# Six more stretches of zero-matmuls in chunks 0 and 1 of a fused attention and SoLU kernel, and five wide ones in place of eighteen narrow ones

## The chip, the cores and the metric

The kernel runs on one core of a Trainium2 chip. A core has five engines that run side by side and wait for each other through semaphores: TensorE (PE in the profile; its weight loads are shown apart as PEld), VectorE (DVE), ScalarE (ACT), GpSimd (POOL) and SyncE (SP). The last two also issue most of the DMA transfers. The metric is the device time of one execution in microseconds; lower is better.

## What is computed

The reference is linear attention with a norm per head, followed by a two-layer network with a SoLU and a layer norm. Batch 8, 8 heads, 576 positions, head width 64, so 4608 tokens of width 512, and 1024 hidden columns:

```python
kv  = einsum('bhsd,bhse->bhde', k, v)
o   = einsum('bhsd,bhde->bhse', q, kv)
x   = o / sqrt(mean(o*o, -1) + 1e-6) * g_norm          # then laid out as (4608, 512)
h   = x @ w_in                                         # (4608, 1024)
u   = h * softmax(h)
ln  = (u - mean(u)) / sqrt(var(u) + 1e-6) * g_ln
out = ln @ w_out                                       # (4608, 512)
```

## The kernel before, in words

The work is cut into nine chunks. Chunks 0 to 7 are 512 positions of one batch each, chunk 8 gathers the last 64 positions of all batches. A chunk goes through these pieces, named in the kernel as `name.chunk.part`:

- `q`, `k`, `v`: loads, issued by POOL (L317). Chunks 0 and 1 come in two halves. The first half of chunk 0 is loaded by SP (L327) and cast by DVE and ACT (L231).
- `qT_mm` (L415): PE turns q; `qT` (L231): a copy of it out of PSUM.
- `kv_mm` (L377): 72 small products of k and v per half; `kv` (L231): copies of the result.
- `o_mm` (L443): 8 products of q and kv; `sq` (L235): ACT squares the result; `s_mm` (L507): one product with `head_mean`, the mean over a head; `ex` (L521 in chunk 0; `ln`, `ex` at L511 and L515 from chunk 1): the reciprocal root on ACT; `x` (L527): DVE multiplies. Each is done for two halves `hf` and two parts `z`, as `s_mm.0.1.0`.
- `h` (L582 in chunks 0 to 3, L611 later): products with `w_in`. Then `exp` on ACT (L589, L619), `u` on DVE (L593, L625), squares and sums on POOL, and `out` (L759): the products with `w_out`, scaled and stored.
- Once per run, `w_mean` (L740) and `w_center` (L745) fold the layer norm into `w_out`, whose two halves POOL loads (L346). `w_in` is loaded at L341.

The order in which every piece is issued is written out by hand, in one list, `ORDER`. The framework adds the waits. Each engine works through its own pieces in this order, so a piece that waits holds up everything behind it on the same engine. PSUM has eight banks; `HOME` gives each PSUM tile (`s.0.0.1`, `h.0.7` and so on) its bank. A tile may be written when every reader of the bank's previous tile is done.

`warm.N` pieces are zero-matmuls: TensorE multiplies a tile of zeros into a PSUM tile that the piece behind it will overwrite. `FILL` lists them as (tile, how many, columns). Those with 512 columns run at L822. `warm.1`, on the tile of q's first turn by PE after the first products of k and v, is 18 transposes of 128 columns (L817). Before the change there are seven such pieces: 19 and 8 wide matmuls ahead of the first data (`warm.6`, `warm.3`, `warm.2`, `warm.0`), `warm.1`, one wide matmul at `warm.4` and one at `warm.5`.

Of the kernel before, what the change touches and what calls it, by code (L numbers as in the profile page):

```python
# [22 lines left out]
o_mm.0.0 q_last.0:act sq.0.0.1 kv.0.1.1 kv.0.1.0 s_mm.0.0.1 sq.0.0.0 ex.0.0.1 o_mm.0.1 sq.0.1.1 sq.0.1.0 g_ln  # L23
s_mm.0.0.0 x.0.0.1 v.1.1 ex.0.0.0 s_mm.0.1.1 ex.0.1.1 x.0.0.0 x.0.1.1 w_out.0 s_mm.0.1.0 qT_mm.1.0 qT.1.0 w_out.1
q.2.0 k.2.0 ex.0.1.0 x.0.1.0 v.2.0 kv_mm.1.0 kv.1.0.1:act kv.1.0.0:act h.0.7.0 table h.0.1.0 warm.5 h.0.4.0 o_mm.1.0
sq.1.0.0 sq.1.0.1 k.3.0 h.0.5.0 g_mean h.0.6.0 h.0.4.1 exp.0.4 u.0.4 usq.0.4 h.0.1.1 exp.0.1 h.0.6.1 u.0.1 usq.0.1
h.0.5.1 exp.0.5 es.0.2 u.0.5 usq.0.5 exp.0.6 u.0.6 h.0.0.0 h.0.0.1 exp.0.0 u.0.0 q.3.0 usq.0.0 s_mm.1.0.1 ln.1.0.1
ex.1.0.1 qT_mm.1.1 qT.1.1 usq.0.6 x.1.0.1 h.0.2.0 h.0.2.1 exp.0.2 u.0.2 s_mm.1.0.0 ln.1.0.0 ex.1.0.0 h.0.7.1 exp.0.7
es.0.3 kv_mm.1.1 kv.1.1.1 kv.1.1.0 x.1.0.0 h.0.3.0 h.0.3.1 exp.0.3 u.0.3 es.0.0 es.0.1 usq.0.3 o_mm.1.1 sq.1.1.1
usq.0.2 u.0.7 usq.0.7 sq.1.1.0 w_mean.0 s_mm.1.1.1 ln.1.1.1 ex.1.1.1 s_mm.1.1.0 ln.1.1.0 v.3.0 w_mean.1 x.1.1.1  # L30
w_center.0 h.1.0.0 h.1.7.0 h.1.3.0 v.5.0 ex.1.1.0 x.1.1.0 w_center.4 h.1.1.0 h.1.2.0 h.1.2.1 exp.1.2 w_center.2
qT_mm.2.1 qT_mm.2.0 h.1.3.1 k.5.0 u.1.2 usq.1.2 w_center.3 qT.2.1:act v.4.0 qT.2.0:act h.1.7.1 exp.1.7 w_center.1
w_center.5 h.1.1.1 exp.1.1 u.1.1 h.1.5.0 h.1.5.1 h.1.4.0 exp.1.5 exp.1.3 h.1.6.0 h.1.6.1 h.1.0.1 exp.1.0 u.1.5 k.4.0
es.1.1 usq.1.5 es.1.0 q.4.0 u.1.7 usq.1.7 h.1.4.1 u.1.0 kv_mm.2.0 kv.2.1.1 exp.1.6 es.1.3 exp.1.4 kv.2.0.0
kv.2.1.0:act u.1.4 k.6.0 w_center.6 u.1.6 kv.2.0.1:act w_center.7 kv.2.1.2:act out.0.2.0 kv.2.0.2:act out.0.3.0
out.0.3.1 out.0.3.2 usq.1.4:act u.1.3 usq.1.3 o_mm.2.0 sums.0 sq.2.0.1 s_mm.2.0.1 es.1.2 sq.2.0.0 v.6.0 s_mm.2.0.0
usq.1.6 ln.2.0.0 ln.2.0.1 ex.2.0.0 turn.0 stats.0 rstd.0 out.0.2.1 out.0.2.2 out.0.2.3 ob.0.2 store.0.2 o_mm.2.1
sq.2.1.0 sq.2.1.1 x.2.0.0 out.0.0.0 out.0.0.1 out.0.0.2 out.0.3.3 ob.0.3:act usq.1.0 store.0.3 out.0.0.3 ob.0.0
store.0.0 ex.2.0.1 s_mm.2.1.0 qT_mm.3.1 kv_mm.3.0 kv.3.0.1 k.7.0 x.2.0.1 ln.2.1.0 v.7.0 kv.3.1.1:act kv.3.1.0
kv.3.0.2:act kv.3.1.2 ex.2.1.0 x.2.1.0 out.0.1.0 out.0.1.1 kv.3.0.0:act s_mm.2.1.1 ln.2.1.1 out.0.1.2 out.0.1.3 ob.0.1  # L40
usq.1.1 ex.2.1.1 h.2.7.0 x.2.1.1 qT_mm.3.0 qT.3.0:act h.2.5.0 q_last.3:act h.2.4.0 h.2.0.0 h.2.0.1 exp.2.0 q_last.1
h.2.3.0 h.2.6.0 h.2.3.1 exp.2.3 h.2.7.1 qT.3.1 u.2.0 kv_mm.5.0 kv.5.1.0 kv.5.0.1:act q.5.0 exp.2.7 kv.5.0.2:act
kv.5.0.0:act h.2.4.1 exp.2.4 store.0.1 kv.5.1.1:act q.6.0 qT.5 u.2.3 u.2.7 kv.5.1.2 h.2.2.0 h.2.2.1 exp.2.2 usq.2.7
h.2.1.0 h.2.1.1 u.2.2 usq.2.0 h.2.6.1 u.2.4 o_mm.3.1 out.1.2.0 usq.2.2 out.1.2.1 exp.2.1 es.2.0 u.2.1 sq.3.1.0 exp.2.6
u.2.6 s_mm.3.1.0 ln.3.1.0 ex.3.1.0 sums.1 turn.1 stats.1 q_last.4 h.2.5.1 sq.3.1.1 out.1.3.0 q_last.2 g_all s_mm.3.1.1
kv_mm.4.0 exp.2.5 x.3.1.0 u.2.5 ln.3.1.1 es.2.1 usq.2.6 kv.4.0.0:act kv.4.0.2 kv.4.1.1 rstd.1 usq.2.5 ob.1.2 kv.4.0.1
ex.3.1.1 x.3.1.1 o_mm.3.0 sq.3.0.0 usq.2.4:act es.2.2 out.1.1.0 usq.2.1 kv.4.1.2:act out.1.3.1 ob.1.3 store.1.3 es.2.3
qT_mm.4.1 qT.4.1 sq.3.0.1 kv.4.1.0:act out.1.0.0 s_mm.3.0.0 ln.3.0.0 ex.3.0.0 out.1.1.1 ob.1.1 s_mm.3.0.1 o_mm.4.1
qT_mm.4.0 ln.3.0.1 ex.3.0.1 x.3.0.0 store.1.2 x.3.0.1 out.1.0.1 qT.4.0 kv_mm.6.0 kv.6.1.1 kv.6.1.0 ob.1.0 sq.4.1.1
store.1.0 kv.6.1.2 kv.6.0.2 s_mm.4.1.1 ln.4.1.1 h.3.5.1 exp.3.5 u.3.5 sq.4.1.0 h.3.2.1 exp.3.2 u.3.2 usq.3.2 h.3.4.1  # L50
exp.3.4 u.3.4 h.3.0.1 kv.6.0.1:act ex.4.1.1 x.4.1.1 exp.3.0 u.3.0 kv.6.0.0 s_mm.4.1.0 ln.4.1.0 h.3.1.1 exp.3.1 usq.3.5
h.3.6.1 kv_mm.7.0 kv.7.1.0 kv.7.0.1:act kv.7.1.2:act usq.2.3 kv.7.0.0:act u.3.1 store.1.1 o_mm.4.0 sq.4.0.0 kv.7.0.2
exp.3.6 kv.7.1.1 h.3.3.1 h.3.7.1 exp.3.3 u.3.3 out.2.2.0 out.2.2.1 es.3.1 sq.4.0.1 s_mm.4.0.1 exp.3.7 es.3.3 u.3.6
ex.4.1.0 x.4.1.0 ln.4.0.1 ex.4.0.1 u.3.7 usq.3.7:act s_mm.4.0.0 ln.4.0.0 ex.4.0.0 x.4.0.1 qT.6 out.2.0.0 sums.2
out.2.3.0 o_mm.5.0 es.3.2 turn.2 stats.2 rstd.2 x.4.0.0 o_mm.5.1 sq.5.1.0 sq.5.0.1 out.2.0.1 usq.3.4 ob.2.0 sq.5.0.0
out.2.3.1 ob.2.2 store.2.2 ob.2.3 s_mm.5.1.0 ln.5.1.0 ex.5.1.0 x.5.1.0 h.4.1.0 expt.4.1.0 s_mm.5.0.0 ln.5.0.0 sq.5.1.1
out.2.1.0 out.2.1.1 ob.2.1 ex.5.0.0 usq.3.0 es.3.0 x.5.0.0 h.4.3.0 expt.4.3.0 usq.3.3 s_mm.5.0.1 ln.5.0.1 ex.5.0.1
usq.3.6 usq.3.1 sums.3 ut.4.3.0 ut.4.1.0 turn.3 store.2.1 s_mm.5.1.1 h.4.2.0 bn.4.3.0 stats.3 q.7.0 qT.7 x.5.0.1
ln.5.1.1 ex.5.1.1 x.5.1.1 expt.4.2.0 out.3.3.0 ut.4.2.0 bn.4.2.0 rstd.3 out.3.3.1 o_mm.6.0 sq.6.2 sq.6.0 ob.3.3:act
ssum.6.0 o_mm.6.1 bn.4.1.0 h.4.2.1 q_last.7 sq.6.3 expt.4.2.1 ut.4.2.1 sq.6.1 out.3.2.0 out.3.2.1 ob.3.2 h.4.3.1  # L60
sred.6.0 expt.4.3.1 h.4.1.1 expt.4.1.1 ssum.6.1 ut.4.3.1 ut.4.1.1 rh.6.0 turnu.4.1 rg.6.0 out.3.0.0 out.3.0.1
ob.3.0:act h.4.0.1 sred.6.1 rg.6.2 o_mm.7.1 rh.6.1 sq.7.1 bn.4.2.1 xt.6.0 xt.6.2 h.4.0.0 expt.4.0.1 expt.4.0.0 rg.6.3
out.3.1.0 sq.7.3 ut.4.0.1 out.3.1.1 ut.4.0.0 ob.3.1:act bn.4.0.0 rg.6.1 xt.6.1 store.3.2 xt.6.3 x.6 turnu.4.0 h.5.2.1
h.5.0.0 ssum.7.1 sred.7.1 expt.5.2.1 ut.5.2.1 expt.5.0.0 ut.5.0.0 h.5.0.1 store.2.0 expt.5.0.1 h.5.1.1 expt.5.1.1
out.4.3.0 h.5.1.0 ut.5.0.1 bn.4.1.1 out.4.3.1 bn.4.3.1 rh.7.1 q_last.6:act expt.5.1.0 rg.7.3 ut.5.1.1 rg.7.1
q_last.5:act qT.8 xt.7.3 xt.7.1 h.5.3.1 expt.5.3.1 bn.4.0.1 o_mm.7.0 ut.5.1.0 ut.5.3.1 out.4.2.0 sq.7.0 sq.7.2 h.5.2.0
# [798 lines left out]
```

## Time and profile before

| | us |
|---|---|
| three runs | 184.80, 184.79, 186.75; median 184.80 |
| the profiled execution, its own time | 186.39 |
| its span in the trace | 184.3 |
| PE busy | 172.2 |
| ACT busy | 135.6 |
| DVE busy | 133.4 |
| POOL busy | 98.1 |
| mean granted TensorE clock | 0.978 |

The profile is of one execution, and its times are counted from the start of the span; 186.39 - 184.3 = 2.1 us lie around the span. In a line of the timeline stand the start, the duration, the engine, the line of the kernel, the operation with its output and inputs, how many instructions were merged, and in brackets the idle time before with what ended it. "issue" there means that the profile shows nothing that the engine waited for. The granted clock is the share of its full speed at which TensorE ran. A matmul's duration includes its way through the array, so that of several in a row the distance between two starts is the price, and not the duration of one.

### The profile page before, as it was taken

What the parts mean: (1) busy time and instruction counts of PE and PEld (TensorE: products, weight loads), DVE (VectorE), ACT (ScalarE), POOL (GpSimd) and SP (SyncE); (2) the same over time, 40 slices, a digit from 0 to 9 for tenths busy, and PEclk for the clock granted to TensorE, in tenths of its full rate; (3) what the DMA queues carried; (4) which work ended last, traced back from release to release, by engine and by line L of the source; (5) the groups of instructions that cost most, each with busy time, mean ns of one, the idle gap of its engine ahead of it and who ended that gap; (6) DMA issues with size and microseconds to landing.
All of it is one profiled execution on the core that took longest, in us unless ns stands there. A gap on an engine that the chain in (4) does not pass through costs nothing.

```text
span 184.3 us, 5088 instructions
## 1 busy us (share of the span) xinstructions
PE 172.2 (93%) x2072; PEld 83.9 (46%) x2072; DVE 133.4 (72%) x277; ACT 135.6 (74%) x279; POOL 98.1 (53%) x112
## 2 busy tenths in 40 slices
...
PEclk9999569999999999999999999999999999999998
...
GB/s 182 292 217 207 207 322 312 208 207 201 208 210 229 270 213 208 208 199 166 215 103 66 177 136 173 55 227 179 219 247 77 252 261 171 230 144 206 215 233 201
DMA packets 56140, 37.10 MB, mean 201 GB/s; under 512 B 37549, under 2 KB 49333, under 8 KB 56117
## 3 DMA queue, kind: packets, MB, share of 16 engines
...
q8 instruction: 16, 0.26, 0.5%
...
## 4 chain that ended last, share of the span: by engine, by line
PE 57%; DVE 9%; DMA 3%; ACT 2%; POOL 1%; issue 1%; POOLq 0%; ACTq 0%
PE out_ps L759 22%; PE h_ps L611 17%; PE h_ps L582 8%; DMA w_sb<-u_sb 3%; DVE bn_sb L631 3%; DVE u_sb L625 2%; PE misc_ps L377 2%; PE misc_ps L693 2%; PE s_ps L507 2%; PE o_ps L443 1%; PE o_ps L457 1%; PE misc_ps L415 1%; POOL es_sb L472 1%; DVE x_sb L527 1%; DVE w_out_sb L745 1%; ACT rst_sb L235 1%
## 5 line engine op out<-in xcount | busy, mean ns | idle before, releaser
L611 PE MATMUL h_ps<-w_in_sb,x_sb 128*128 128x512 bf16 x160 | 38.0, 379 | 0.4 <-DVE usq_sb L495 0.4
L759 PE MATMUL out_ps<-w_out_sb,w_sb 128*128 128x512 bf16 (+1 forms) x168 | 36.9, 369 | 0.3 <-DMA w_sb<-u_sb 0.3
L237 POOL TENSOR_TENSOR usq_sb<-u_sb 128x512 bf16<-128x512 bf16 x29 | 29.7, 1041 | 12.2 <-PE s_ps L507 6.5
L582 PE MATMUL h_ps<-x_sb,w_in_sb 128*128 128x512 bf16 x128 | 32.3, 396 | 2.6 <-DVE x_sb L527 2.6
L619 ACT ACTIVATE e_sb<-h_ps,zero_t 128x512 f32<-128x512 f32 x40 | 27.2, 686 | 8.6 <-PE h_ps L611 7.9
L759 PE MATMUL out_ps<-w_out_sb,u_sb 128*128 128x512 bf16 x128 | 31.0, 379 | 0.0
L593 DVE TENSOR_TENSOR u_sb<-h_ps,e_sb 128x512 bf16<-128x512 f32 x32 | 20.8, 684 | 11.0 <-ACT e_sb L589 10.9
L625 DVE TENSOR_TENSOR u_sb<-h_ps,e_sb 128x512 bf16<-128x512 f32 x40 | 26.0, 679 | 1.6 <-ACT e_sb L619 1.6
L631 DVE BATCH_NORM_STATS2 bn_sb<-u_sb 128x6 f32<-128x512 bf16 x40 | 25.8, 680 | 0.2
L759 PEld LDWEIGHTS <-w_sb 128*128 128x128 bf16 x168 | 16.3, 98 | 18.7 <-DMA w_sb<-u_sb 0.8
L527 DVE SCALAR_TENSOR_TENSOR x_sb<-o_ps,g_cols,rst_sb 128x512 bf16<-128x512 f32 x24 | 18.8, 795 | 7.9 <-ACT rst_sb L515 3.8
L589 ACT ACTIVATE e_sb<-h_ps,zero_t 128x512 f32<-128x512 f32 x32 | 20.6, 690 | 4.7 <-PE h_ps L582 4.6
L611 PEld LDWEIGHTS <-x_sb 128*128 128x128 bf16 x160 | 15.4, 97 | 19.0 <-issue 1.2
L606 POOL TENSOR_TENSOR es_sb<-e_sb 128x512 bf16<-128x512 f32 x16 | 20.3, 1275 | 2.2 <-ACT e_sb L589 2.2
L582 PEld LDWEIGHTS <-w_in_sb 128*128 128x128 bf16 x128 | 12.3, 100 | 17.9 <-issue 6.1
L235 ACT ACTIVATE osq_sb<-o_ps,zero_t 128x512 bf16<-128x512 f32 x24 | 15.5, 681 | 5.5 <-PE o_ps L443 5.4
L759 PEld LDWEIGHTS <-u_sb 128*128 128x128 bf16 x128 | 11.8, 98 | 14.1 <-issue 0.8
L488 POOL TENSOR_TENSOR lss_sb<-rh_sb,g_all 128x512 f32<-128x512 f32 x12 | 12.2, 1041 | 7.9 <-ACT rh_sb L484 7.9
L472 POOL TENSOR_TENSOR es_sb<-rst_sb 128x512 f32<-128x512 bf16 x6 | 6.9, 1155 | 15.4 <-ACT rst_sb L235 9.0
L511 ACT ACTIVATE lss_sb<-s_ps,eps_t 128x512 f32<-128x512 f32 x20 | 13.6, 684 | 1.7 <-PE s_ps L507 1.6
L515 ACT ACTIVATE rst_sb<-lss_sb,zero_t 128x512 f32<-128x512 f32 x20 | 14.5, 723 | 0.5
L231 DVE CAST kvd<-misc_ps 64x128 bf16<-64x128 f32 (+1 forms) x23 | 6.3, 286 | 8.7 <-PE misc_ps L377 7.4
...
## 6 DMA issues: line engine op xcount, KB each, us to landing
...
w_sb<-in_moe_w_out_dram POOLq DMA_DIRECT2D x2, 1024.0 KB, 15.4
...
```

What stands on the lines that cost most here:

```text
L235: nc.scalar.activation(out=dst, in_=src, func=AF.Square, bias=zero_t[:, :])
L237: on[engine].tensor_tensor(out=dst, in0=src, in1=src, op=MUL)
L527: nc.vector.scalar_tensor_tensor(out=t[:, z, 2 * hf:2 * hf + 2].rearrange("p a (vt w) -> p w (a vt)", w=2), in0=T["o", c, hf, z].rearrange ...
L582: nc.tensor.matmul(bank(("h", c, f), [128, 512])[:, :], w_in_sb[:, dt, f * 128:(f + 1) * 128], T["x", c][:, :, dt, :], start=(dt == 0), st ...
L589: nc.scalar.activation(out=t[:, f % 2, :], in_=T["h", c, f][:, :], func=AF.Exp, bias=zero_t[:, :])
L593: nc.vector.tensor_tensor(out=t[:, f, :], in0=T["h", c, f][:, :], in1=T["e", c, f // 2][:, f % 2, :], op=MUL)
L606: on[engine].tensor_tensor(out=t[:, n, :], in0=e[:, 0, :], in1=e[:, 1, :], op=ADD)
L611: nc.tensor.matmul(bank(("h", c, m, g), [128, 512])[:, :], x[:, NP * (m ^ 2 * odd(c, dt)) + dt, :] if c in TOKA else x[:, m // 2 ^ odd(c, ...
L619: nc.scalar.activation(out=t[:, g, :], in_=T["h", c, m, g][:, :], func=AF.Exp, bias=zero_t[:, :], accum_out=se[:, m, g:g + 1])
L625: nc.vector.tensor_tensor(out=t[:, m, g * 512:(g + 1) * 512], in0=T["h", c, m, g][:, :], in1=T["e", c, m][:, g, :], op=MUL)
L631: nc.vector.bn_stats(out=t[:, m, g, :], in_=T["u", c][:, m, g * 512:(g + 1) * 512])
L759: nc.tensor.matmul(bank(key, [128, d_model])[:, cols], T["w", c][:, m, f, :] if c in TOKS else T["u", c][:, f, m * 128:(m + 1) * 128], w_o ...
```

## The change

Six pieces `warm.7` to `warm.12` are added, each ahead of a piece that waits: 4 wide matmuls ahead of `s_mm.0.0.1`, 2 ahead of `s_mm.0.1.1`, 1 ahead of `s_mm.0.1.0`, 4 ahead of `h.0.7.0`, 1 ahead of `s_mm.1.1.1` and 3 ahead of `h.1.1.0`. `warm.1` becomes 5 wide matmuls and no longer needs the identity. The order of all other pieces stays word for word. The homes of many PSUM tiles are renumbered. The tiles of the k and v products are declared as whole banks, and the copies read the same part of them as before.

```diff
 ORDER (only the places with a new word; the rest is the same sequence)
-... kv.0.1.1 kv.0.1.0 s_mm.0.0.1 sq.0.0.0 ex.0.0.1 o_mm.0.1 ...
+... kv.0.1.1 kv.0.1.0 warm.7 s_mm.0.0.1 sq.0.0.0 ex.0.0.1 o_mm.0.1 ...
-... ex.0.0.0 s_mm.0.1.1 ex.0.1.1 x.0.0.0 x.0.1.1 w_out.0 s_mm.0.1.0 qT_mm.1.0 ...
+... ex.0.0.0 warm.8 s_mm.0.1.1 ex.0.1.1 x.0.0.0 x.0.1.1 w_out.0 warm.12 s_mm.0.1.0 qT_mm.1.0 ...
-... kv.1.0.1:act kv.1.0.0:act h.0.7.0 table h.0.1.0 warm.5 h.0.4.0 o_mm.1.0 ...
+... kv.1.0.1:act kv.1.0.0:act warm.9 h.0.7.0 table h.0.1.0 warm.5 h.0.4.0 o_mm.1.0 ...
-... w_mean.0 s_mm.1.1.1 ... w_center.4 h.1.1.0 ...
+... w_mean.0 warm.10 s_mm.1.1.1 ... w_center.4 warm.11 h.1.1.0 ...

-FILL = {0: ("s.warm", 19, 512), 1: ("misc.qT.0.0", 18, 128), 2: ("o.0.0.1", 5, 512), ...}
+FILL = {0: ("s.warm", 19, 512), 1: ("misc.qT.0.0", 5, 512), 2: ("o.0.0.1", 5, 512), ...
+        7: ("s.0.0.1", 4, 512), 8: ("s.0.1.1", 2, 512), 9: ("h.0.7", 4, 512), 10: ("s.1.1.1", 1, 512),
+        11: ("h.1.1", 3, 512), 12: ("s.0.1.0", 1, 512)}

 def kv_mm, kv_copy:
-    bank(kv_key(b, x, w), [128, 2, D])          ... T[kv_key(b, x, part)][:, :, :]
+    bank(kv_key(b, x, w), [128, 8, D])          ... T[kv_key(b, x, part)][:, 0:2, :]

 def warm(key, n, cols):
     if kind == "qT":
-        t = bank(key, [128, 2, 4, 128], BF16)
-        for i in range(n):
-            nc.tensor.transpose(t[:, 0, i % 4, :], zeros[:, 0:128], ident[:, :])
-        return
+        flat = bank(key, [128, 2, 4, 128], BF16).rearrange("p n y t -> p (n y t)").bitcast(FP32)
...
     for _ in range(n):
         nc.tensor.matmul(flat[:, 0:cols], zeros[:, :], zeros[:, None, :].to_broadcast([128, cols // 128, 128]), start=True, stop=True)
```

Followed through the list, the renumbering gives eight tiles another predecessor in their bank: `s.0.0.1` now follows `kv.0.1.1` in place of `kv.0.1.0`, `o.0.1.0` the other way round, `h.0.1` follows `o.0.1.0`, `o.1.0.0` follows `qT.1.0`, `o.1.0.1` follows `kv.1.0.1`, `h.0.5` follows `s.0.1.0`, `h.1.2` follows `o.1.1.0` and `qT.2.1` follows `s.1.0.0`.

More of the change, by code (lines that the diff above doesn't have):

```diff
@@ L22 @@
 kv.0.0.1:act warm.1 k.1.0 qT.0.1:act gs w_in.0 w_in.1 k.1.1 ld.q q.0.0 qT_mm.0.0 warm.4 q.1.1 qT.0.0 kv_mm.0.1 turn_g
[L23 to L66, printed above, removed]
@@ new lines @@
+s_mm.0.0.0 x.0.0.1 v.1.1 ex.0.0.0 warm.8 s_mm.0.1.1 ex.0.1.1 x.0.0.0 x.0.1.1 w_out.0 warm.12 s_mm.0.1.0 qT_mm.1.0
+qT.1.0 w_out.1 q.2.0 k.2.0 ex.0.1.0 x.0.1.0 v.2.0 kv_mm.1.0 kv.1.0.1:act kv.1.0.0:act warm.9 h.0.7.0 table h.0.1.0
+warm.5 h.0.4.0 o_mm.1.0 sq.1.0.0 sq.1.0.1 k.3.0 h.0.5.0 g_mean h.0.6.0 h.0.4.1 exp.0.4 u.0.4 usq.0.4 h.0.1.1 exp.0.1
+h.0.6.1 u.0.1 usq.0.1 h.0.5.1 exp.0.5 es.0.2 u.0.5 usq.0.5 exp.0.6 u.0.6 h.0.0.0 h.0.0.1 exp.0.0 u.0.0 q.3.0 usq.0.0
+s_mm.1.0.1 ln.1.0.1 ex.1.0.1 qT_mm.1.1 qT.1.1 usq.0.6 x.1.0.1 h.0.2.0 h.0.2.1 exp.0.2 u.0.2 s_mm.1.0.0 ln.1.0.0
@@ new lines @@
+h.1.6.1 h.1.0.1 exp.1.0 u.1.5 k.4.0 es.1.1 usq.1.5 es.1.0 q.4.0 u.1.7 usq.1.7 h.1.4.1 u.1.0 kv_mm.2.0 kv.2.1.1 exp.1.6
+es.1.3 exp.1.4 kv.2.0.0 kv.2.1.0:act u.1.4 k.6.0 w_center.6 u.1.6 kv.2.0.1:act w_center.7 kv.2.1.2:act out.0.2.0
+kv.2.0.2:act out.0.3.0 out.0.3.1 out.0.3.2 usq.1.4:act u.1.3 usq.1.3 o_mm.2.0 sums.0 sq.2.0.1 s_mm.2.0.1 es.1.2
+sq.2.0.0 v.6.0 s_mm.2.0.0 usq.1.6 ln.2.0.0 ln.2.0.1 ex.2.0.0 turn.0 stats.0 rstd.0 out.0.2.1 out.0.2.2 out.0.2.3
+ob.0.2 store.0.2 o_mm.2.1 sq.2.1.0 sq.2.1.1 x.2.0.0 out.0.0.0 out.0.0.1 out.0.0.2 out.0.3.3 ob.0.3:act usq.1.0
@@ new lines @@
+h.2.2.1 exp.2.2 usq.2.7 h.2.1.0 h.2.1.1 u.2.2 usq.2.0 h.2.6.1 u.2.4 o_mm.3.1 out.1.2.0 usq.2.2 out.1.2.1 exp.2.1
+es.2.0 u.2.1 sq.3.1.0 exp.2.6 u.2.6 s_mm.3.1.0 ln.3.1.0 ex.3.1.0 sums.1 turn.1 stats.1 q_last.4 h.2.5.1 sq.3.1.1
+out.1.3.0 q_last.2 g_all s_mm.3.1.1 kv_mm.4.0 exp.2.5 x.3.1.0 u.2.5 ln.3.1.1 es.2.1 usq.2.6 kv.4.0.0:act kv.4.0.2
+kv.4.1.1 rstd.1 usq.2.5 ob.1.2 kv.4.0.1 ex.3.1.1 x.3.1.1 o_mm.3.0 sq.3.0.0 usq.2.4:act es.2.2 out.1.1.0 usq.2.1
+kv.4.1.2:act out.1.3.1 ob.1.3 store.1.3 es.2.3 qT_mm.4.1 qT.4.1 sq.3.0.1 kv.4.1.0:act out.1.0.0 s_mm.3.0.0 ln.3.0.0
@@ new lines @@
+ex.3.0.0 out.1.1.1 ob.1.1 s_mm.3.0.1 o_mm.4.1 qT_mm.4.0 ln.3.0.1 ex.3.0.1 x.3.0.0 store.1.2 x.3.0.1 out.1.0.1 qT.4.0
+kv_mm.6.0 kv.6.1.1 kv.6.1.0 ob.1.0 sq.4.1.1 store.1.0 kv.6.1.2 kv.6.0.2 s_mm.4.1.1 ln.4.1.1 h.3.5.1 exp.3.5 u.3.5
+sq.4.1.0 h.3.2.1 exp.3.2 u.3.2 usq.3.2 h.3.4.1 exp.3.4 u.3.4 h.3.0.1 kv.6.0.1:act ex.4.1.1 x.4.1.1 exp.3.0 u.3.0
+kv.6.0.0 s_mm.4.1.0 ln.4.1.0 h.3.1.1 exp.3.1 usq.3.5 h.3.6.1 kv_mm.7.0 kv.7.1.0 kv.7.0.1:act kv.7.1.2:act usq.2.3
+kv.7.0.0:act u.3.1 store.1.1 o_mm.4.0 sq.4.0.0 kv.7.0.2 exp.3.6 kv.7.1.1 h.3.3.1 h.3.7.1 exp.3.3 u.3.3 out.2.2.0
```

121 lines of the change are left out of this document (75 added, 46 removed).

## The prediction, made before the result was known

> **What bounds the kernel now.** I read the page first (busy shares, then the granted clock in 40 slices of 4.6 us), then busy time by window, then the timeline of the early part.
>
> ```profile
> span 184.3 us, 5088 instructions
> PE 172.2 (93%) x2072; PEld 83.9 (46%) x2072; DVE 133.4 (72%) x277; ACT 135.6 (74%) x279; POOL 98.1 (53%) x112
> PEclk9999569999999999999999999999999999999998
> ```
>
> TensorE is busy for 172 of 184 us. Its clock is whole but for the fifth and sixth slice. The windows carry start and end, length, then busy us of PE, PEld, DVE, ACT, POOL, then the clock:
>
> ```profile
> 12.17:15.58 3.41, 2.27 (x91) 1.18 (x88) 1.25 (x4) 1.79 (x3) 1.47 (x2) 1.00 1.21 207
> 15.58:19.00 3.42, 2.09 (x29) 1.07 (x31) 1.50 (x3) 2.47 (x5) 1.48 (x2) 1.00 1.14 212
> 19.00:22.41 3.41, 2.33 (x75) 1.46 (x71) 2.59 (x5) 2.40 (x4) 0.74 (x1) 0.50 1.15 206
> 22.41:25.82 3.41, 3.41 (x16) 0.96 (x15) 0.00 (x0) 0.99 (x2) 1.48 (x2) 0.50 1.22 255
> 80.00:110.00 30.00, 30.00 (x435) 14.82 (x434) 24.31 (x51) 28.68 (x56) 17.24 (x18) 1.00 0.80 151
> ```
>
> The clock is at half from 19.00 to 25.82 us. It fell behind a stretch in which TensorE was busy for 2.09 of 3.42 us, held behind one with 2.27 of 3.41, and came back behind one that was full. From 80 to 110 us TensorE has no gap, so what it does earlier in the first 60 us is still earlier there. What matters lies between 10 and 40 us:
>
> ```profile
> 10.53 1.18 PE L817 MATMUL misc_ps<-ident,zeros 128*128 128x128 bf16 x18
> 11.66 0.62 PE L415 MATMUL misc_ps<-ident,q_sb 128*128 128x128 bf16 x8
> 13.32 0.41 PE L443 MATMUL o_ps<-qT_sb,kvd 64*64 64x256 bf16 x8
> 14.52 0.38 PE L507 MATMUL s_ps<-osq_sb,head_mean 128*128 128x512 bf16 x1 [0.79 <-ACT osq_sb L235]
> 14.83 0.40 PE L443 MATMUL o_ps<-qT_sb,kvd 64*64 64x256 bf16 x5
> 16.07 0.30 PE L443 MATMUL o_ps<-qT_sb,kvd 64*64 64x256 bf16 x3 [0.83 <-issue]
> 16.30 0.39 PE L507 MATMUL s_ps<-osq_sb,head_mean 128*128 128x512 bf16 x1
> 17.15 0.38 PE L507 MATMUL s_ps<-osq_sb,head_mean 128*128 128x512 bf16 x1 [0.46 <-ACT osq_sb L235]
> 17.72 0.38 PE L507 MATMUL s_ps<-osq_sb,head_mean 128*128 128x512 bf16 x1 [0.20 <-ACT osq_sb L235]
> 18.88 1.11 PE L377 MATMUL misc_ps<-v_sb,k_sb 64*64 64x64 bf16 x71 [0.19 <-ACT rst_sb L521]
> 21.07 1.86 PE L582 MATMUL h_ps<-x_sb,w_in_sb 128*128 128x512 bf16 x4 [1.08 <-DVE x_sb L527]
> 22.73 0.63 PE L822 MATMUL h_ps<-zeros 128*128 128x512 bf16 x1
> 23.16 1.06 PE L582 MATMUL h_ps<-x_sb,w_in_sb 128*128 128x512 bf16 x2
> 24.14 0.64 PE L443 MATMUL o_ps<-qT_sb,kvd 64*64 64x256 bf16 x8
> 24.71 4.16 PE L582 MATMUL h_ps<-x_sb,w_in_sb 128*128 128x512 bf16 x16
> 33.41 1.19 PE L740 MATMUL out_ps<-w_sb,g_mean 128*128 128x512 f32 x4
> 34.91 0.38 PE L507 MATMUL s_ps<-osq_sb,head_mean 128*128 128x512 bf16 x1 [0.31 <-ACT osq_sb L235]
> 39.20 1.46 PE L582 MATMUL h_ps<-x_sb,w_in_sb 128*128 128x512 bf16 x6 [0.95 <-DVE x_sb L527]
> ```
>
> The six new pieces stand in the bracketed waits of 0.79, 0.46, 0.20, 1.08, 0.31 and 0.95 us. The seventh gap, 0.83 us inside `o_mm.0.1`, has no releaser: five of eight products ran, and the sixth came 1.1 us later.
>
> **The change, part by part.** The price of one wide matmul at full clock, and of `o_mm`, from the chain of what ended last:
>
> ```profile
> 59.72 3.45 PE h_ps L582 x16
> 66.57 0.34 PE o_ps L443 x8
> ```
>
> A wide one is 3.45 / 16 = 0.216 us. Zero-matmuls have the same shape.
>
> *warm.1.* Eighteen transposes fill 10.53 to 11.66, 1.13 us; five wide ones take 1.08. The next piece waits for its q behind them either way. Zero.
>
> *The renumbered banks.* Of the eight tiles with another predecessor, `s.0.0.1` and `o.0.1.0` swap two copies that both end by 13.76 (first row below), `h.0.1` and `h.1.2` now need an x that the product of h just ahead of them on PE awaits already, and the others need an earlier reader. Zero. The whole-bank tiles read and write what they did. Zero.
>
> ```profile
> 13.27 0.49 DVE L231 CAST kvd<-misc_ps 128x128 bf16<-128x128 f32 x2 [0.26 <-PE misc_ps L377]
> 18.28 1.47 DVE L527 SCALAR_TENSOR_TENSOR x_sb<-o_ps,g_cols,rst_sb 128x512 bf16<-128x512 f32 x2 [1.84 <-ACT rst_sb L521]
> 19.64 0.69 DVE L231 COPY qT_sb<-misc_ps 128x1024 bf16<-128x1024 bf16 x1
> 20.23 0.79 DVE L527 SCALAR_TENSOR_TENSOR x_sb<-o_ps,g_cols,rst_sb 128x512 bf16<-128x512 f32 x1
> 16.41 1.26 ACT L235 ACTIVATE osq_sb<-o_ps,zero_t 128x512 bf16<-128x512 f32 x2 [0.78 <-PE o_ps L443]
> 19.17 0.69 ACT L521 ACTIVATE rst_sb<-s_ps,eps_t 128x512 f32<-128x512 f32 x1 [0.34 <-DVE x_sb L527]
> ```
>
> *The fills themselves*, at full clock. `warm.7`: 4 x 0.216 = 0.86 from 13.73 (end of `o_mm.0.0`) is 14.59, against a start of `s_mm.0.0.1` at 14.52: 0.07 late. `warm.8`: 0.43 into 0.46. `warm.12`: 0.22 into 0.20, 0.02 late. `warm.9`: 0.86 into 1.08. `warm.10`: 0.22 into 0.31. `warm.11`: 0.65 into 0.95. Behind each waits only the piece that the gap belonged to. Sum +0.05 to +0.1; I take +0.05, since the ACT work behind `s_mm.0.0.1` is queued behind a square anyway.
>
> *The fall of the clock.* With the fills, the two thin windows hold 2.27 + 0.86 = 3.13 and 2.09 + 0.65 = 2.74 us of work, both above the 2.27 that did not bring the fall. So I expect no fall. Its price in place: from 21.07 to 24.14 seven wide matmuls took 3.07 us where 7 x 0.216 = 1.51 would do (1.56 saved); `o_mm.1.0` took 24.71 - 24.14 = 0.57 where 0.34 would do (0.23); of 24.71 to 25.82, 1.11 us, half goes (0.55). Sum 2.34 us. That `kv_mm.1.0` was slowed too (71 products from 18.88) costs nothing: the x of DVE at 20.23 + 0.79 was the later one.
>
> The runs give another bound. 184.79 and 184.80 agree to 0.01, and 186.39 and 186.75 lie 1.6 and 2.0 above. I take the lower pair as executions where the fall lay in the waits of 15 to 21 us and cost little. Then what of 2.34 reaches the end is 186.39 - 184.80 = 1.59. It is the row nearest to the question, and I take it; 2.34 stays as the other end.
>
> *The seventh gap.* In the very stretch before it, one DMA of kind "instruction" runs (window 13.6 to 14.8 of the DMA view, packets, MB, share):
>
> ```profile
> q8 instruction: 1, 0.02, 5.1%
> ```
>
> I read the gap as TensorE out of instructions: the sixth weight load had been done, and its matmul came last in what had been fetched. The change takes 13 zero pairs (weight load and matmul) out of `warm.1` and puts 4 in at `warm.7`, 9 pairs or 18 instructions less ahead of this point. The last 5 instructions of `o_mm.0.1`, the next three `s_mm` (6) and their fills (6) are 17. So what had been fetched now reaches to q's turn of chunk 1, which starts past 17 us. Then `o_mm.0.1` ends some 0.8 us earlier, ACT does not idle 0.78 before 16.41, and its next pieces and DVE's x, up to the last x at 20.23, move up with it, less 0.03 to 0.07 for the fill. I take -0.75; bounds 0 (the gap stays) and -0.83. What is late next: the landing of `w_in`, and later of `w_out`.
>
> ```profile
> 20.03 0.74 POOL L317 DMA_DIRECT2D k_sb<-in_k_dram  x1 [1.74 <-DMA w_in_sb<-in_moe_w_in_dram]
> 22.52 0.74 POOL L317 DMA_DIRECT2D v_sb<-in_v_dram  x1 [1.75 <-DMA w_in_sb<-in_moe_w_in_dram]
> 13.97 0.76 POOL L346 DMA_DIRECT2D w_sb<-in_moe_w_out_dram  x1 [1.00 <-DVE g_cols L288]
> DMA to landing us min/median/max: 15.3/15.4/15.5
> ```
>
> The halves of `w_in` are there by 20.03 and 22.52. `h.0.7.0` would start at 21.07 - 0.75 = 20.3, and the first product of the second half five wide matmuls, `o_mm` and two more later, at 20.3 + 9 x 0.216 + 0.34 = 22.6. The first half of `w_out` lands at 13.97 + 15.3 = 29.3 and is used at 33.41, which may move 3.1 us. Both fit.
>
> *Sum.* The profiled execution's own time is 186.39 (span 184.3). 186.39 - 1.59 - 0.75 + 0.05 = 184.1 us. Against the median of the runs, 184.80, this is -0.7 us or 0.4%.
>
> A rule that speaks against the change: the Trainium skill, page "TensorE: Matmul & The Clock Gate", section "Why this matters for your kernels", has the clock drop only after TensorE idles for more than about 3 us. By it, no gap here (1.08 at most) would drop the clock, the fills would be idle work, and the sum would keep the 1.59. The trace disagrees: the clock was 0.50 behind such gaps. The section "What's actually happening" has a free-running window of 3.41 us, which would let the fall lie elsewhere in each execution; that the fall lasted 6.82 us agrees with two of them.
>
> **The rivals.**
>
> *A. All of the fall reaches the end, and the lower pair paid for a part of it as well.* For it: the fall's price in place is 2.34, and later loads have slack. Against it: two runs that agree to 0.01 look like a floor. 186.39 - 2.34 - 0.75 + 0.05 = 183.35; with the waits at 34.91 and 39.20 shrinking too, by up to 0.9, down to 182.5.
>
> *B. The instruction gap moves along, or is something else.* For it: only one such gap exists, so its cause is inferred. 186.39 - 1.59 + 0.05 = 184.85: no change.
>
> *C. Slower: zeros do not hold the clock.* If work on zeros or small bursts does not count, the fall stays, and the fills lie in it at 3.07 / 7 = 0.44 us each. `warm.9` then runs 1.75 us from the end of `kv_mm.1.0` (18.88 + 1.11 = 19.99) to 21.74, past 21.07 by 0.67: 186.39 + 0.67 = 187.1. It decides the median once most executions have the fall between 19 and 21. Against it: the 19 zero-matmuls of the start stand ahead of a whole clock until 19.00.
>
> **How the numbers follow.** Forecast 0.50, A 0.27, B 0.13, C 0.10. The likeliest gives 184.1 us. The range reaches into A down to 182.8, leaving out some 0.08 below, and over B to 185.4, leaving out C's 0.10. Faster by over 1% (about what a measurement of this kernel can tell from no change) means under 182.95: half of A, 0.14. Slower by over 1% means over 186.65: C, 0.10. Within 1%: 0.76.
>
> **What would show it.** In the profile of the changed kernel: a granted clock of 1.00 from 10 to 40 us (if it falls, the step on the clock is wrong, and C is near); `o_mm.0.1` as eight products in one piece and ACT's squares near 15.7 and not 16.41 (if the gap sits there still, B); the first h near 20.3; the starts of `s_mm.0.0.1` and `h.0.7.0` right behind their last fill would show a fill too long. A span below 181.5 would mean that the early time is carried whole, A.

## The result and the profile after

The changed kernel takes 183.34 us (median of 16 runs, 182.62 to 184.6), the kernel before 185.74 us in 16 runs taken beside them (184.25 to 187.73): a ratio of 0.9885, interval 0.985 to 0.992. A second set of 12 runs (a set is a number of kernels run side by side on one chip) gave 183.92 us and 0.9949, 0.991 to 0.9987. The two intervals only just meet, so the gain by ratio, 1.2% in one set and 0.5% in the other, is not known more closely. The ratio leaves out the slowest runs of the kernel before, so it lies a little nearer to one than the quotient of the two medians. The three runs from which the prediction started (184.80) lay at the low side of this kernel's spread, and that spread turned out to be the main thing to explain.

The profiled execution of the changed kernel took 184.51 us, 2 us less than the 186.39 of the one before. First its page: the span, the busy shares, and the granted clock in 40 slices.

```profile
span 182.4 us, 5075 instructions
PE 171.9 (94%) x2057; PEld 83.7 (46%) x2074; DVE 133.5 (73%) x277; ACT 135.6 (74%) x279; POOL 98.0 (54%) x112
PEclk9999999999999999999999999999999999999997
```

The 5 and 6 in the clock's row of before are gone. The 7 at the end is a drop of the clock at 180.26 us, behind the last matmul; the kernel before has one too, at 182.84. Next the same kernel's timeline of TensorE, start and length in front, the wait in brackets:

```profile
10.93 1.25 PE L824 MATMUL misc_ps<-zeros 128*128 128x512 bf16 x5
...
13.93 0.41 PE L444 MATMUL o_ps<-qT_sb,kvd 64*64 64x256 bf16 x8
14.27 1.04 PE L824 MATMUL s_ps<-zeros 128*128 128x512 bf16 x4
15.14 0.38 PE L508 MATMUL s_ps<-osq_sb,head_mean 128*128 128x512 bf16 x1
15.45 0.41 PE L444 MATMUL o_ps<-qT_sb,kvd 64*64 64x256 bf16 x8
...
16.03 0.59 PE L824 MATMUL s_ps<-zeros 128*128 128x512 bf16 x2
16.88 0.38 PE L508 MATMUL s_ps<-osq_sb,head_mean 128*128 128x512 bf16 x1 [0.26 <-ACT osq_sb L236]
...
19.31 1.04 PE L824 MATMUL h_ps<-zeros 128*128 128x512 bf16 x4
20.80 1.02 PE L583 MATMUL h_ps<-x_sb,w_in_sb 128*128 128x512 bf16 x4 [0.46 <-DVE x_sb L528]
...
36.71 1.46 PE L583 MATMUL h_ps<-x_sb,w_in_sb 128*128 128x512 bf16 x6 [0.30 <-DVE x_sb L528]
...
140.44 2.75 PE L612 MATMUL h_ps<-w_in_sb,x_sb 128*128 128x512 bf16 x12 [0.43 <-DVE usq_sb L496]
...
172.02 5.37 PE L760 MATMUL out_ps<-w_out_sb,w_sb 128*128 128x512 bf16 x32 [0.34 <-DMA w_sb<-u_sb]
```

`o_mm.0.1`, at 15.45, is eight products in one piece; the 5 and 3 of before, with 0.83 us between them, are gone. The first four `h` take 1.02 us where they took 1.86 at half clock. Two rows of the kernel before are needed to compare the end:

```profile
143.07 2.75 PE L611 MATMUL h_ps<-w_in_sb,x_sb 128*128 128x512 bf16 x12 [0.42 <-DVE usq_sb L495]
...
174.58 5.37 PE L759 MATMUL out_ps<-w_out_sb,w_sb 128*128 128x512 bf16 x32 [0.27 <-DMA w_sb<-u_sb]
```

The time comes in two steps and is then kept. `o_mm.0.0` starts 0.61 later than before (13.93 against 13.32; a part of the reason is in the last section). The first `h` is nevertheless 0.27 earlier (20.80 against 21.07): 0.88 gained on the way, of which 0.83 is the gap. The piece that stood at 39.20 is at 36.71, 2.49 earlier and so another 2.22: the clock. At 140.44 the lead is 2.63, at the last group of `out` 2.56. From there to the end of the span this execution took 182.4 - 172.02 = 10.4 us and the one before 184.3 - 174.58 = 9.7, so 1.9 is left.

### The profile page after: what moved, and what is told of

The parts are those of the page before. It is cut to its first block, busy times and chain, and to the rows that moved or that the text cites. A ratio compares the mean times of both kernels' runs of the same rounds, so it can differ in the third digit from the quotient of the medians.

```text
span 182.4 us, 5075 instructions
## 1 busy us (share of the span) xinstructions
PE 171.9 (94%) x2057; PEld 83.7 (46%) x2074; DVE 133.5 (73%) x277; ACT 135.6 (74%) x279; POOL 98.0 (54%) x112
## 4 chain that ended last, share of the span: by engine, by line
PE 56%; DVE 12%; DMA 3%; ACT 1%; issue 1%
PE out_ps L760 22%; PE h_ps L612 17%; PE h_ps L583 8%; DVE bn_sb L632 4%; DVE u_sb L626 4%; DMA w_sb<-u_sb 3%; PE misc_ps L378 2%; PE misc_ps L694 2%; PE s_ps L508 2%; PE o_ps L444 1%; PE misc_ps L416 1%; DVE x_sb L528 1%; PE o_ps L458 1%; DVE w_out_sb L746 1%; DVE usq_sb L496 1%
## 5 line engine op out<-in xcount | busy, mean ns | idle before, releaser
L612 PE MATMUL h_ps<-w_in_sb,x_sb 128*128 128x512 bf16 x153 | 37.0, 379 | 0.8 <-DVE usq_sb L496 0.4
L583 PE MATMUL h_ps<-x_sb,w_in_sb 128*128 128x512 bf16 x128 | 30.4, 379 | 1.4 <-DVE x_sb L528 1.4
L760 PE MATMUL out_ps<-w_out_sb,u_sb 128*128 128x512 bf16 x120 | 30.4, 379 | 0.5
```

What stands on the lines that cost most here:

```text
L583: nc.tensor.matmul(bank(("h", c, f), [128, 512])[:, :], w_in_sb[:, dt, f * 128:(f + 1) * 128], T["x", c][:, :, dt, :], start=(dt == 0), st ...
L612: nc.tensor.matmul(bank(("h", c, m, g), [128, 512])[:, :], x[:, NP * (m ^ 2 * odd(c, dt)) + dt, :] if c in TOKA else x[:, m // 2 ^ odd(c, ...
L760: nc.tensor.matmul(bank(key, [128, d_model])[:, cols], T["w", c][:, m, f, :] if c in TOKS else T["u", c][:, f, m * 128:(m + 1) * 128], w_o ...
```

## The experiments

The theory after the result: TensorE runs dry of instructions inside `o_mm.0.1`, 18 instructions fewer ahead of it cure that, the clock falls because the stretch is thin, and what is early there stays early to the end. The rivals: the gap is a wait of another kind; the fills alone hold the clock and the gap is worth nothing; early time is lost again further on. The medians of all runs, each beside runs of the kernel before on the same chip (12 runs of each kernel; the last row is a single run):

| kernel | us (range) | ratio to before, interval | gap in o_mm.0.1 | runs with a fall |
|---|---|---|---|---|
| fills, 18 narrow ahead | 185.02 (183.83 to 186.47) | 0.9995, 0.9953 to 1.0038 | 0.83 | 0 of 12 |
| five wide ahead, no new fills | 184.12 (183.28 to 185.12) | 0.995, 0.9918 to 0.9982 | none | 2 of 12 |
| before with 9 narrow | 184.02 (183.37 to 186.24) | 0.9945, 0.991 to 0.9979 | none | 1 of 12 |
| after with 14 narrow ahead | 184.51 (183.81 to 185.43) | 0.995, 0.9919 to 0.9981 | 0.72 | 0 of 12 |
| after, again | 183.92 (182.76 to 184.78) | 0.9949, 0.991 to 0.9987 | none | 0 of 12 |
| after without warm.7, 8, 12 | 183.67 (182.69 to 184.27) | 0.9924, 0.9889 to 0.996 | none | 4 of 12 |
| after without warm.9, 10, 11 | 183.32 (182.83 to 184.76) | 0.9936, 0.989 to 0.9982 | none | 0 of 12 |
| after, warm.0 of 14 | 183.14 (182.74 to 183.54) | 0.9909, 0.9875 to 0.9943 | none | 0 of 12 |
| after, warm.7 of 8 | 184.83 (183.83 to 186.1) | 1.0023, 0.9989 to 1.0057 | none | 0 of 12 |
| after with 14 narrow, again | 184.83 (183.57 to 185.81) | 1.0029, 0.9997 to 1.0061 | 0.83 | 0 of 12 |
| warm.0 of 14, no warm.9, 10, 11 | 183.68 (183.39 to 185.11) | 0.997, 0.9938 to 1.0003 | none | 1 of 12, perhaps 2 |
| before, one more run | 183.66 | (single run) | 0.74 | none |

The first four stand beside runs of before with a median of 185.88, the next four beside 185.68, the three after them beside 184.95; these are three sets. In all 14 traces the granted clock changes only after whole multiples of 3.41 us, and a stretch of 3.41 us between two such moments is called a window here. One window at half clock is 3.41 x 0.5 / 184 = 0.0093 of the mean granted clock that each run lists, and the 98 runs of the kernel before in the three sets do lie in steps of about that size. A mean below 0.99 is counted as a fall; in the traces the drop behind the last matmul alone brings the mean down to 0.993.

| mean clock of the run | runs of before | median us |
|---|---|---|
| 0.99 and above | 21 | 183.89 |
| 0.98 to 0.99 | 29 | 185.03 |
| 0.97 to 0.98 | 32 | 186.24 |
| below 0.97 | 16 | 187.25 |

Each step costs 1.0 to 1.2 us. The kernel before lost at least one window in 77 of 98 runs, the changed one in none of 28. The border at 0.99 is not sharp: two runs of the first row (185.88 and 186.00, both at 0.991) have the time of a run that lost a window, and so has one run of the kernel with both edits (185.11 at 0.991).

### The gap: which instructions, and what it is worth

*Fills with the eighteen narrow ones kept*, as transposes; the change without its second part:

```diff
-1: ("misc.qT.0.0", 5, 512)
+1: ("misc.qT.0.0", 18, 128)
```

> The changed kernel with warm.1 as eighteen transposes again. Theory (the 0.83 us gap in o_mm.0.1 is TensorE out of instructions; the count ahead of it decides): 8 instructions more than before stand ahead of o_mm.0.1, so the gap is back, after the first of its products instead of the fifth, and ends about 2.3 us after the start of the instruction DMA; the clock stays whole; the time is 0.6 to 0.9 us above the changed kernel, about 184.1. Rival (the gap came with the clock's fall or by chance): no gap, time of the changed kernel, 183.3.

The gap came back, at another place. The timeline of TensorE in this kernel, there and later:

```profile
14.69 0.29 PE L444 MATMUL o_ps<-qT_sb,kvd 64*64 64x256 bf16 x1
15.82 0.41 PE L444 MATMUL o_ps<-qT_sb,kvd 64*64 64x256 bf16 x7 [0.83 <-issue]
...
105.17 1.69 PE L760 MATMUL out_ps<-w_out_sb,u_sb 128*128 128x512 bf16 x7 [1.24 <-issue]
```

Four pairs of weight load and matmul more stand ahead (`warm.7`), and the gap comes four products earlier: after one product and not after five. It sits at a number of instructions, not at a piece of work. The kernel also shows a second one, at 105 us. The clock held in all 12 runs, and still the ratio is 0.9995. The six runs of the kernel before in this set that kept the clock have a median of 183.89, 1.1 us less; the second gap, 1.24, would account for that, but one profile does not show it for all runs.

*Five wide ones without the new fills*, the change without its first part:

```diff
-o_mm.0.0 ... warm.7 s_mm.0.0.1 ... warm.8 ... warm.12 ... warm.9 ... warm.10 ... warm.11 ...
+o_mm.0.0 ... s_mm.0.0.1 ...
```

> Before with warm.1 as five wide matmuls, none of the six new pieces. Theory: 26 instructions fewer ahead of o_mm.0.1, so no gap in it; the clock still falls to a half for two windows (6.8 us) somewhere between 15 and 26 us in most executions; the time is 0.6 to 0.9 us under the kernel before, 184.9 by medians. Rival (wide matmuls at 11 us hold the clock by themselves): no fall, 183.3.

*The kernel before with nine transposes in place of eighteen*, the smallest edit that takes instructions away:

```diff
-1: ("misc.qT.0.0", 18, 128)
+1: ("misc.qT.0.0", 9, 128)
```

> Before with nine transposes in warm.1 in place of eighteen; nothing wide is added and TensorE has 0.56 us less of zero work. Theory: 18 instructions fewer, no gap in o_mm.0.1, so the time is 0.6 to 0.9 us under the kernel before although there is less work for the clock, which still falls. Rival (the gap has another cause): the gap stays, the time is that of before.

The two rows of the first, then one of the second:

```profile
15.17 0.41 PE L444 MATMUL o_ps<-qT_sb,kvd 64*64 64x256 bf16 x8
...
20.53 1.02 PE L583 MATMUL h_ps<-x_sb,w_in_sb 128*128 128x512 bf16 x4 [1.43 <-DVE x_sb L528]
```

```profile
15.03 0.41 PE L443 MATMUL o_ps<-qT_sb,kvd 64*64 64x256 bf16 x8
```

No gap in either, and this is the surprise: without a single new fill, with the wait of 1.43 us ahead of the first `h` left open, the clock fell in only 3 of 24 runs, against 29 of 35 of the kernel before beside them. Most of what the change is worth can be had by leaving nine transposes out. The first of these kernels has the banks of the changed one and the second those of the kernel before, so the renumbering made no difference that shows.

*The changed kernel with fourteen narrow zero-matmuls* in place of the five wide ones: 14 + 4 pairs, the 18 of before.

```diff
-1: ("misc.qT.0.0", 5, 512)
+1: ("misc.qT.0.0", 14, 128)
```

> The changed kernel with warm.1 as fourteen matmuls of 128 columns, so that exactly as many instructions stand ahead of o_mm.0.1 as before. Theory: the gap is back in its old place, after five products of o_mm.0.1; the clock is whole; 0.6 to 0.9 us above the changed kernel, about 184.1. Rival: no gap, 183.3.

```profile
15.49 0.40 PE L444 MATMUL o_ps<-qT_sb,kvd 64*64 64x256 bf16 x5
16.61 0.30 PE L444 MATMUL o_ps<-qT_sb,kvd 64*64 64x256 bf16 x3 [0.72 <-issue]
```

Five and three again, as in the kernel before. This kernel ran once more in another set:

> The kernel with fourteen narrow matmuls in warm.1 once more, beside other variants of the changed kernel on the same chip. Theory: gap at the same instruction, clock whole in all runs, 0.5 to 0.9 us above the variants without the gap.

```profile
14.42 0.40 PE L444 MATMUL o_ps<-qT_sb,kvd 64*64 64x256 bf16 x5
15.66 0.30 PE L444 MATMUL o_ps<-qT_sb,kvd 64*64 64x256 bf16 x3 [0.83 <-issue]
```

In every profile that shows the gap, 449 records of TensorE stand ahead of the matmul behind it (443 weight loads and matmuls, 6 of TensorE's sequencer), and the gap ends 2.3 to 2.4 us after the start of a DMA of kind "instruction" on queue 8 (13.72 and 16.07 before; 13.51 and 15.82; 14.32 and 16.61; 13.30 and 15.66; and 13.65 and 15.92 in the last run below). In the nine profiles without the gap the record that has 449 ahead of it starts 2.8 to 4.3 us after that DMA, so by the same delay it was there in time. That it is a shortage of instructions is as good as shown. Its price with the fills in place: 184.83 against the changed kernel's 183.92 on the same chip, 0.9 us, though from two sets. The medians do not fix this price, since the ratio of the kernel with fourteen narrow ones was 0.995 in one set and 1.0029 in the other.

### Is early time carried to the end?

*A known delay*: `warm.7` of eight, four wide matmuls too many, 0.86 us.

```diff
-7: ("s.0.0.1", 4, 512)
+7: ("s.0.0.1", 8, 512)
```

> The changed kernel once more, to stand beside the three others on the same chip. Theory: no fall of the clock in any run, median about 1.2% under the median of before.

> The changed kernel with 8 in place of 4 matmuls in warm.7: four more at 0.216 us, 0.86 us later for s_mm.0.0.1, half of which the squares on ACT ahead of it hide. Theory (early time is carried whole to the last matmul, TensorE being full from 60 us on): the first h, the h at 56 us and the last out stand later by the same 0.4 to 0.9 us, and the time is 0.4 to 0.9 us above the changed kernel. Rival (a third of early time is absorbed, as the forecast took it): the delay at the last out is two thirds of that at the first h or less.

First the changed kernel in its second profile, then the one with the delay. Both had their clock at full from 4.5 us on, and their starts agree (`o_mm.0.0` at 12.97 and 12.90):

```profile
19.85 1.02 PE L583 MATMUL h_ps<-x_sb,w_in_sb 128*128 128x512 bf16 x4 [0.46 <-DVE x_sb L528]
...
55.23 0.59 PE L583 MATMUL h_ps<-x_sb,w_in_sb 128*128 128x512 bf16 x2 [0.60 <-DVE x_sb L528]
...
139.49 2.75 PE L612 MATMUL h_ps<-w_in_sb,x_sb 128*128 128x512 bf16 x12 [0.43 <-DVE usq_sb L496]
...
170.94 5.37 PE L760 MATMUL out_ps<-w_out_sb,w_sb 128*128 128x512 bf16 x32 [0.21 <-DMA w_sb<-u_sb]
```

```profile
13.25 1.90 PE L824 MATMUL s_ps<-zeros 128*128 128x512 bf16 x8
...
20.64 1.02 PE L583 MATMUL h_ps<-x_sb,w_in_sb 128*128 128x512 bf16 x4 [0.46 <-DVE x_sb L528]
...
56.02 0.59 PE L583 MATMUL h_ps<-x_sb,w_in_sb 128*128 128x512 bf16 x2 [0.59 <-DVE x_sb L528]
...
140.23 2.75 PE L612 MATMUL h_ps<-w_in_sb,x_sb 128*128 128x512 bf16 x12 [0.42 <-DVE usq_sb L496]
...
171.69 5.37 PE L760 MATMUL out_ps<-w_out_sb,w_sb 128*128 128x512 bf16 x32 [0.22 <-DMA w_sb<-u_sb]
```

Behind by 0.79, 0.79, 0.74 and 0.75 us: what is lost in the first 20 us arrives at the end all but whole. The two executions took 183.18 and 184.04 us, 0.86 apart; the medians, from two sets, are 0.91 apart. The rival, that early time is lost again further on, falls.

### Which fills are needed?

The first kernel leaves out `warm.7`, `warm.8` and `warm.12`, the second `warm.9`, `warm.10` and `warm.11`:

```diff
-... kv.0.1.0 warm.7 s_mm.0.0.1 ... ex.0.0.0 warm.8 s_mm.0.1.1 ... w_out.0 warm.12 s_mm.0.1.0 ...
+... kv.0.1.0 s_mm.0.0.1 ... ex.0.0.0 s_mm.0.1.1 ... w_out.0 s_mm.0.1.0 ...
```

```diff
-... kv.1.0.0:act warm.9 h.0.7.0 ... w_mean.0 warm.10 s_mm.1.1.1 ... w_center.4 warm.11 h.1.1.0 ...
+... kv.1.0.0:act h.0.7.0 ... w_mean.0 s_mm.1.1.1 ... w_center.4 h.1.1.0 ...
```

> The changed kernel without warm.7, warm.8 and warm.12; the wide warm.1 and the later fills stay. Theory (the missing instructions made the thin stretch that dropped the clock; once they are there in time, the fills are almost idle work): no gap in o_mm.0.1, a mean clock of 0.985 or less in at most one run of five, a median within 0.5 us of the changed kernel. Rival (these fills hold the clock): falls in most runs, a median 1 to 2 us above it.

> The changed kernel without warm.9, warm.10 and warm.11. Theory: no fall of the clock, a median within 0.3 us of the changed kernel: with the clock whole they lie in waits. Rival (the stretch from 19 to 21 us with its wait of 1.4 us, or the one from 34 to 39, drops the clock): falls, 1 us or more above it.

Neither half is slower than the changed kernel beside it (183.92), and both lie within 0.6 us of it. Without the first three, 4 of 12 runs lost one window, at 183.74 to 184.27; without the last three, none. The first three hold the clock in some runs, for some 0.4 us each time (183.98 is the median of those four, 183.54 of the other eight); the last three can't be told from idle work. Both hold for a kernel without the instruction gap; with it, only all six together were run.

### Less filling at the start

The start has 19 wide zero-matmuls in `warm.0`. In the first profile after, PE's first turn of q (`qT_mm.0.1`) starts at 9.69, right behind them and without a wait: its data had been there, and the fills held it up. The products of k and v follow at 10.22, the copy of their result on DVE at 11.06, the cast of q's other half at 11.27, and the second turn (`qT_mm.0.0`) at 12.27:

```profile
9.69 0.61 PE L416 MATMUL misc_ps<-ident,q_sb 128*128 128x128 bf16 x8
...
12.27 0.62 PE L416 MATMUL misc_ps<-ident,q_sb 128*128 128x128 bf16 x8
```

```diff
-0: ("s.warm", 19, 512)
+0: ("s.warm", 14, 512)
```

> The changed kernel with 14 in place of 19 zero-matmuls in warm.0. In its profile the last of them ends at 9.54 us, while q's first half has landed at 8.15. Theory: the turn of q starts 1.0 us earlier, the second turn and the products of k and v about 0.9, so the first h comes 0.8 to 0.9 us earlier and the time is 0.6 to 0.9 us lower. Rival (the clock then rises later or falls, or the loads set the pace): no gain.

183.14 us with runs from 182.74 to 183.54, a spread of 0.8 where the changed kernel has 2.0: 0.8 less than the changed kernel beside it, and the lowest of all. The rows that now set the two turns of q, two of TensorE and one of DVE:

```profile
8.14 0.62 PE L416 MATMUL misc_ps<-ident,q_sb 128*128 128x128 bf16 x8 [0.90 <-DMA q_sb<-in_q_dram]
11.23 0.62 PE L416 MATMUL misc_ps<-ident,q_sb 128*128 128x128 bf16 x8 [0.57 <-DVE q_sb L232]
```

```profile
10.41 0.76 DVE L232 CAST q_sb<-usq_sb 128x1152 bf16<-128x1152 f32 x1 [0.59 <-DMA usq_sb<-in_q_dram]
```

The first turn waits for its load, the second for the cast on DVE, and the cast for the load of the other half at 10.41; by these rows still less filling would buy nothing, though it was not run. The expected 0.8 to 0.9 us at the first `h` is there against the first profile of the changed kernel (19.94 and 20.80), but not against the second (19.85), in which the clock rose early and the cast began at 10.45 behind all 19. So in these profiles the gain is not a shift of every execution: what goes is the late start of those whose clock rises late, as the last section shows. Both ideas together:

> The changed kernel with 14 matmuls in warm.0 and without warm.9, warm.10 and warm.11. Theory: these fills are idle work once the instructions are there, so no fall, no gap, and the time of the kernel with the shorter warm.0, 2.5 us under before or a little better. Rival: the wait of 1.4 us ahead of the first h, with nothing in it, drops the clock in some runs: a mean clock of 0.985 and about 1 us more in those.

183.68 us, 0.997 with an interval up to 1.0003, and one run or two lost a window. The two edits together are no better than the first alone.

### What did the kernel before do in its good runs?

> The kernel before, unchanged, profiled once more. The question is what the executions of it that kept the clock (21 of 98, median 183.89 us) looked like. Theory: in them the instruction gap inside o_mm.0.1 did not occur, which is why the clock held; so a profile at a mean clock of 0.99 or more should show eight products in one piece there and a time near 183.9, and one at 0.98 or less (about four in five executions) the gap of 0.8 us after the fifth product and a stretch at half clock behind it, one window of 3.41 us for each 0.0093 of the mean. Rival: the gap is always there and only the phase of the clock's window decides; then a profile that kept the clock still shows 5 and 3 products. In either case a fallen profile says whether the fall lies at 19 us again or elsewhere; a fall that starts before 17 us, in the waits, with a time near 185.0 would speak for the prediction's reading of the lower pair.

This run kept the clock (another beside it, not profiled, took 187.08 us at a mean of 0.968, which makes three windows). Its page, timeline and three windows (cut at the times at which its clock's windows begin):

```profile
span 181.5 us, 5071 instructions
PEclk9999999999999999999999999999999999999999
```

```profile
14.78 0.40 PE L443 MATMUL o_ps<-qT_sb,kvd 64*64 64x256 bf16 x5
15.92 0.30 PE L443 MATMUL o_ps<-qT_sb,kvd 64*64 64x256 bf16 x3 [0.74 <-issue]
...
20.93 1.02 PE L582 MATMUL h_ps<-x_sb,w_in_sb 128*128 128x512 bf16 x4 [1.43 <-DVE x_sb L527]
...
36.82 1.46 PE L582 MATMUL h_ps<-x_sb,w_in_sb 128*128 128x512 bf16 x6 [0.95 <-DVE x_sb L527]
...
140.53 2.75 PE L611 MATMUL h_ps<-w_in_sb,x_sb 128*128 128x512 bf16 x12 [0.43 <-DVE usq_sb L495]
```

```profile
12.06:15.48 3.42, 2.33 (x92) 1.23 (x89) 1.25 (x4) 1.80 (x4) 1.41 (x2) 1.00 1.21 207
15.48:18.89 3.41, 2.12 (x33) 1.10 (x36) 1.54 (x3) 2.52 (x5) 1.48 (x2) 1.00 1.13 212
18.89:22.30 3.41, 1.98 (x78) 1.18 (x69) 2.56 (x5) 2.29 (x4) 0.74 (x2) 1.00 1.16 208
```

My theory, that the gap is absent in such runs, fell: 5 and 3 products, 0.74 us. The rival stands: the gap was there and the clock held. The windows say why that can be. In the first profile the window 15.58 to 19.00 held 2.09 us of work and the clock fell; here, cut 0.1 us earlier, it holds 2.12 and the clock did not. The kernel before seems to sit on an edge, where a small shift of the windows decides; two profiles cannot show that. Busy time does not draw this edge: the third window here holds still less, 1.98, and the clock held behind it too. Columns may: summed over the matmuls that start in a window (the last number of each shape), the window before the fall has 4288 columns, the fewest of all some 700 windows in the 14 traces, the window of 2.12 here has 4544, and every other one between 12 and 26 us at full clock 5120 or more. With one fall in the traces this is a reading and no proof.

This run is also the cleanest price of the fall, since it is the same kernel without it. `h` at 36.82 against 39.20: 2.38 us earlier, with `o_mm.0.0` starting at 13.27 against 13.32. So 2.33 came from two windows at half clock, and the prediction had worked out 2.34 in place. At 140.53 against 143.07 it is 2.54, and in the time 183.66 against 186.39, 2.73.

## Why the prediction was right, and where it was not

The median fell where rival A's sum had put it (183.35), 0.8 us below the forecast and inside the range; it was A that came true, and not the forecast's own case. That the agreement is as close as 0.01 us is luck: A's sum starts from one execution that had lost two windows, and the second set's median is 183.92. By the ratio of 0.9885 the result also lies among the outcomes faster by over 1%, to which the prediction gave 0.14, because the kernel before took 185.74 beside it and not 184.80.

- **warm.1, the renumbered banks, the fills: zero to +0.05.** Right. `s_mm.0.0.1` starts 1.21 us after `o_mm.0.0` (15.14 and 13.93), where it was 1.20 before (14.52 and 13.32); `warm.7` ends just then, at 14.27 + 4 x 0.216 = 15.13. Ahead of `h.0.7.0` a wait of 0.46 is left, so `warm.9` delays nothing.
- **The instruction gap: -0.75.** Right in mechanism, and in place about right: from `o_mm.0.0` to the first `h` 6.87 us against 7.75, and 7.66 in the second profile of the kernel before; that is 0.8 to 0.9. Squares on ACT, awaited near 15.7 where they started at 16.41, start at 16.15 and follow the reciprocal root ahead of them (L522) without idling; all of this execution is 0.61 late:

```profile
15.56 0.69 ACT L522 ACTIVATE rst_sb<-s_ps,eps_t 128x512 f32<-128x512 f32 x1
16.15 1.26 ACT L236 ACTIVATE osq_sb<-o_ps,zero_t 128x512 bf16<-128x512 f32 x2
```

- **Zero-matmuls hold the clock.** Right: no fall in 28 runs, and rival C is out. The reason was given too simply, though. Fills alone hold it (no fall in 36 runs of the kernels that had fills and gap), and so, nearly, does the absence of the gap alone (3 of 24 fell).
- **The fall of the clock: -1.59.** This step failed. The prediction said: "I take the lower pair as executions where the fall lay in the waits of 15 to 21 us and cost little", and so took 1.59 as what of 2.34 reaches the end. The runs show no such cheap fall. They lie on steps of 1.0 to 1.2 us for each window, and 184.79 and 184.80 agree with the step of one window (median 185.03, from 184.38); the clock of those two runs is not listed, and where their window lay no profile shows. An execution with no fall takes 183.66. The 2.34 that the prediction had worked out from the rows is carried whole (2.33 at 36.82 us), and the floor to subtract it from was not 184.80. Two equal runs were read as a floor where they were one step of a stair.
- **What would show it.** "A span below 181.5 would mean that the early time is carried whole": 182.4 in the first profile, 181.0 in the second. The test was badly chosen, because the span also holds the start and the last stores, which vary by more than half a microsecond each; the lead at 36 us, at 140 us and at the last product is the better measure.
- **The rule on idle gaps.** The prediction weighed the rule of the Trainium skill (page "TensorE: Matmul & The Clock Gate", section "Why this matters for your kernels") by which the clock holds as long as TensorE has no idle gap of more than about 3 us. The runs still disagree: the fall at 19.00 us came behind gaps of at most 0.83 us, since the wait of 1.08 us lies behind its start, and in the second profile of the same kernel the clock held through a wait of 1.43 us.
- **The landing of `w_in`.** The prediction reckoned with nine wide matmuls up to the first product of the second half and named seven in words; the list has eleven and `o_mm.1.0`. What it concluded holds: no wait for `w_in` shows in the profile after.

Two things stay open. First, the edge itself: by busy time it cannot be drawn, since windows with 2.08 us (without `warm.9`, 10 and 11) and 1.79 us (with both edits) kept the clock where 2.09 lost it. By columns it would lie between 4288 and 4544, but what the clock counts was not measured. Second, the gap's 0.8 us at the level of the medians: the kernel before in runs that kept the clock (183.89) is only 0.55 slower than the changed kernel in its first set and no slower than in its second (183.92), while gap against no gap among the kernels with fills is 0.6 to 1.1 (184.51 to 185.02 against 183.92, over several sets, and the 185.02 with a second gap). The last stores scatter by as much (the span ends 9.5 us behind the start of the last group of `out` in the second profile of before, 10.4 in the first profile after), and runs that kept the clock are no random sample of starts.
